# Moving the factor of an eighth from the keys into the exponential of a sparse attention kernel

## The chip, the cores and the metric

The kernel runs on one core of a Trainium2 chip. The metric is the device time of one execution in microseconds (us). The core has five engines that work side by side, each with its own queue of instructions: TensorE (PE in the views, with PEld for its weight loads), VectorE (DVE), ScalarE (ACT), GpSimd (POOL) and SyncE (SP). DMA transfers are issued from the queues of SP, ACT and POOL. An instruction that has to wait holds back everything behind it on its own queue.

## The reference

Four batches of 768 positions go through attention with 8 heads of 64 and a block-sparse mask (blocks of 32; each block of queries sees its neighbours, the first and the last block, and three sampled blocks), and then through a feed-forward layer of 512 to 2048 to 512 with a gate.

```python
scores = (1.0 / np.sqrt(64)) * np.matmul(q, k.transpose(0, 1, 3, 2))      # an eighth
scores = np.where(mask, scores, -1000000000.0)
scores = scores - np.max(scores, axis=-1, keepdims=True)
attn = np.exp(scores)
attn = attn / (np.sum(attn, axis=-1, keepdims=True) + 1e-09)
out = np.matmul(attn, v)                       # then x = out, heads side by side
h = x @ w_in
g = h * erf(softplus(h))
result = g @ w_out
```

## The kernel before

**Units.** A batch is cut into 15 units of attention: 11 of kind "m" (two blocks of queries each, all heads; the names `s_m`, `less_m`, `pf_m`, `p_m`, `pT_m`) and 4 of kind "f" (the first and the last block of queries against all keys, one pair of heads each; the names with `_f`). So there are 44 and 16 in all. `scores` (line 612) has TensorE multiply queries and keys into one PSUM tile `s`. `soft_max` (line 557) has VectorE take the negated maximum `less` of each group of `s`: four numbers per partition for an m unit, one for an f unit. `soft_exp` (line 565) has ScalarE compute exp(s + less) into `pf`, four instructions for an m unit and one for an f unit, and then a copy of `pf` in half precision, `p`; `soft_low` (line 601) gives the rest of it, and a transposing DMA issued by SP turns it for `values`, which multiplies with the values on TensorE into `po`.

**The feed-forward steps.** Between the units run 96 steps: `h` on TensorE, then on ScalarE a chain of five activations on `x` and `y`, on VectorE `y<-y,x`, on ScalarE `y<-y`, on VectorE `y<-y,h` (the gate, which is the last reader of `h` and frees one of its three buffers) and two instructions for `g`; then `o` on TensorE, and twice in eight steps an activation that takes `o` out to SBUF (`wi<-o`, `wo<-o`). From the fourth of these steps on, the engines keep the order in which the program is written (`held`, line 29 onward). Ahead of that, a stretch of some 130 us in which weights are decoded and the first units run, a scheduler puts the instructions of PE, ACT and DVE in an order of its own from its own estimate of times; SP and POOL keep the program's order all along.

**The next batch.** While a batch runs, `behind` (line 852) prepares the next one, piece by piece, once per unit. On POOL this is, in this order: the maximum over partitions for the values' scale (`allm_v`, a PARTITION_ALL_REDUCE), two gathers for the running batch, a MEMSET of `vn`, then four times `kx<-kr` with two more MEMSETs between them. `kr` is one pair of heads' keys as they come from memory; `load_k` (line 123) issues its DMA from ACT's queue into a buffer named `pf`, of which there are two, shared with the exponentials' `pf`. `order_k` (line 134) writes the keys block by block into `kx` and multiplies them by an eighth: ACT does it for batch 0, POOL for the other three. The second `kr` of a batch takes the buffer of the first one, so ACT's DMA issue for it stands in ACT's queue until POOL's first `kx<-kr` is done, and all of ACT's work behind it stands too.

All engine instructions are issued through one helper, so that they carry line 48 in the views; a group is told by its tiles.

Of the kernel before, what the change touches and what calls it, by code (L numbers as in the profile page):

```python
# [12 lines left out]
AF = mybir.ActivationFunctionType  # L13
ALU = mybir.AluOpType
# [17 lines left out]
def sparse_attention_moe(ctx: ExitStack, tc: tile.TileContext, qT, kT, v, sampled, w_in, w_out, out):  # L32
# [7 lines left out]
    class InOrder:  # L40
# [15 lines left out]
    pe, act, dve, pool, sp = (  # L56
        InOrder(e, queued if e in (nc.sync, nc.gpsimd) else held) for e in (nc.tensor, nc.scalar, nc.vector, nc.gpsimd, nc.sync)
    )
    B, H, D, S = qT.shape
# [38 lines left out]
    kxs = {}  # L98
# [35 lines left out]
    def order_k(b, pr):  # L134
        if b not in kxs:
            kxs[b] = ld.tile([P, NB, HP, BLOCK], F32, tag="kx", name=f"kx_{b}", bufs=2)
        kr = krs.pop((b, pr)).rearrange("p (n c) -> p n c", c=BLOCK)
        if b == 0:
            act.activation(kxs[b][:, :, pr, :], kr, AF.Copy, scale=D**-0.5)
        else:  # L140
            pool.tensor_scalar(kxs[b][:, :, pr, :], kr, D**-0.5, None, ALU.mult)

# [412 lines left out]
    def soft_max(unit):  # L557

        s, groups, width = softs[unit]
        tag = "_".join(str(x) for x in unit)  # L560
        less = st.tile([P, 4], F32, tag="less", name=f"less_{tag}")[:, :groups]
        dve.tensor_reduce(less, s.rearrange("p (g w) -> p g w", w=width), AX.X, ALU.max, negate=True)
        softs[unit] += (less,)

    def soft_exp(unit, early=False):

        s, groups, width, less = softs[unit]
        tag = "_".join(str(x) for x in unit)
        n = groups * width
        pf = at.tile([P, 1024], F32, tag="pf", name=f"pf_{tag}", bufs=2)[:, :n]  # L570
        for g in range(groups):
            c = slice(g * width, (g + 1) * width)
            act.activation(pf[:, c], s[:, c], AF.Exp, bias=less[:, g : g + 1])
        if early:
            softs[unit] = (s, groups, width, pf)
            return
        p2 = at.tile([P, 2048], F16, tag="p2", name=f"p2_{tag}", bufs=2)[:, : 2 * n]
        p3 = p2.rearrange("p (g a w) -> p g a w", a=2, w=width)
        pf3 = pf.rearrange("p (g w) -> p g w", w=width)
        act.activation(p3[:, :, 0], pf3, AF.Copy, scale=P_SCALE)  # L580
        softs[unit] = (p2, p3, pf3, n)
# [270 lines left out]
    def behind(m):  # L852

        for c in range(1, B):
            e = m - v_from[c]
            if e in (0, 6):
                load_v(c, 0)
            if e in (1, 3):
                max_v(c, e // 2)
            if e == 4:  # L860
                scale_v(c)
            if e in (4, 5):
                split_v(c, 1, e - 4)
            if e in (7, 8):
                split_v(c, 0, e - 7)
            if e == 8:
                have_v.add(c)
            n = m - k_from[c]
            if 1 <= n < 5:
                order_k(c, n - 1)  # L870
            if 0 <= n < 4:
                load_k(c, n)
            if n == 4:
                have_k.add(c)
# [35 lines left out]
    for pr in range(HP):  # L910
        order_k(0, pr)
# [26 lines left out]
    for begun in range(FIRST):  # L938
        with tc.high_priority():
            if begun >= 2:  # L940
                place = seen(units[begun - 2])
                values(*place)
                used_values(place)
                norm(*place)
                turn(*place, True)
            unit = units[begun]
            scores(unit)
            used_keys(unit)
            soft_max(unit)
            next_queries(begun)  # L950
            soft_exp(unit, True)
            soft_turn(unit)
        gathers()
        later(3)
        if 0 < begun < B:
            zero_rows(begun)
        if begun < 4:
            behind(begun)
# [16 lines left out]
    for m in range(len(groups) + FF_LAG):  # L975
# [39 lines left out]
        if unit:  # L1015
            soft_max(unit)
# [4 lines left out]
        if unit:  # L1021
            soft_exp(unit)
# [42 lines left out]
```

## Time and profile before

| | us |
|---|---|
| median of 3 runs | 784.99 |
| the three runs | 794.81, 779.62, 784.99 |
| the profiled execution | 783.25 |
| its span, first to last instruction | 781.5 |
| PE busy | 685.4 (88%) |
| ACT busy | 591.5 (76%) |
| DVE busy | 570.1 (73%) |
| POOL busy | 219.0 (28%) |
| mean granted TensorE clock | 0.962 of full speed |

The span is what the traced instructions cover; 1.75 us of the execution's 783.25 us lie outside it. Busy shares are means over stages with different limits, so the sections below go by stretches. In a row of the timeline the first number is the start, the second the duration, both in us; brackets at its end give the idle time of that engine just before and what ended it.

### The profile page before, as it was taken

Reading aid. Unit: us, or ns where it says so; the run is one execution under the profiler, and the core shown is the slowest. Engines: PE = TensorE matmul, PEld = TensorE weight load, DVE = VectorE, ACT = ScalarE, POOL = GpSimd, SP = SyncE. Lnnn points to the kernel's source line nnn. Section 1 sums busy time; section 2 is a strip of 40 time slices with the busy share of each in tenths; the row PEclk is TensorE's granted clock in tenths of the full one; section 3 lists DMA queues with packets and bytes.
Section 4 is the critical chain, followed back from the end, with each engine's and each line's share of the span. In section 5 each row is a group of like instructions: output and inputs, shape, how many; then the busy total and the mean of one; then the engine's idle time right before and its main releaser. Section 6 shows DMA issues by size and latency. Waiting matters only on the chain.

```text
span 781.5 us, 24790 instructions
## 1 busy us (share of the span) xinstructions
PE 685.4 (88%) x10400; PEld 449.5 (58%) x10400; DVE 570.1 (73%) x1062; ACT 591.5 (76%) x1023; POOL 219.0 (28%) x413
## 2 busy tenths in 40 slices
PE   1438578879969999899899999899899999999997
PEld 0313346556646666566566666566566666666663
DVE  6985998977748787587768877767767777664553
ACT  2546689859857887688788876888878888787774
POOL 3025523223444322222433332232533320000000
PEclk9967889999989999999999999999999999999999
DMA  9999635996499999862997997745988777221000
GB/s 318 408 276 269 194 96 112 225 205 169 120 217 185 198 178 214 198 168 56 204 199 153 231 200 143 198 112 139 223 161 190 165 139 163 56 52 25 8 28 27
DMA packets 188047, 129.35 MB, mean 166 GB/s; under 512 B 137760, under 2 KB 160928, under 8 KB 186912
## 3 DMA queue, kind: packets, MB, share of 16 engines
q1 hardware_dynamic: 173584, 84.50, 51.3%
q10 hardware_dynamic: 8464, 25.43, 10.1%
q0 software_dynamic: 5888, 17.84, 9.3%
q8 instruction: 81, 1.33, 0.7%
q14 instruction: 30, 0.25, 0.1%
HBM read 82.81 MB, written 12.95 MB: 123 GB/s over the span
## 4 chain that ended last, share of the span: by engine, by line
PE 65%; issue 9%; DMA 8%; ACT 7%; DVE 5%; POOL 4%; SPq 1%; ACTq 1%; POOLq 0%; DVEq 0%
PE h L48 28%; PE o L48 25%; PE s_m L48 5%; PE po_None L48 3%; ACT x L48 3%; DMA wo<-in_w_in_dram 2%; POOL vbuf L48 2%; PE s_f L48 2%; DVE room L48 1%; DMA kr<-in_kT_dram 1%; ACT y L48 1%; DMA raw<-in_w_out_dram 1%; PE po L48 1%; DVE wo L48 1%; DMA pT_f<-p_f 1%
## 5 line engine op out<-in xcount | busy, mean ns | idle before, releaser
L48 PE MATMUL h<-xT,wi 128*128 128x256 f16 x2304 | 272.7, 276 | 9.4 <-DVE y L48 9.4
L48 PE MATMUL o<-wo,g 128*128 128x512 f16 x1152 | 267.9, 383 | 5.4 <-ACT wi L48 5.1
L48 PEld LDWEIGHTS <-wi 128*128 128x128 f16 x2304 | 223.6, 99 | 51.0 <-issue 11.0
L48 ACT ACTIVATE x<-x 128x512 f32<-128x512 f32 x288 | 181.2, 630 | 8.9
L48 PEld LDWEIGHTS <-g 128*128 128x128 f16 x1152 | 110.1, 98 | 134.8 <-issue 17.1
L48 POOL DMA_INDIRECT vbuf<-vtab,idx x88 | 96.1, 1092 | 242.6 <-PE po_None L48 152.1
L48 DVE SCALAR_TENSOR_TENSOR y<-y,x 128x512 f32<-128x512 f32 x96 | 67.7, 705 | 90.2 <-ACT x L48 90.2
L48 ACT ACTIVATE x<-h,isg 128x512 f32<-128x512 f32 x96 | 65.2, 679 | 65.2 <-PE h L48 51.9
L48 POOL COPY kbuf<-kx 128x128 f32 (+1 forms) x280 | 86.8, 355 | 34.4 <-PE s_m L48 27.8
L48 ACT ACTIVATE y<-y 128x512 f32<-128x512 f32 x96 | 59.6, 621 | 32.7 <-DVE y L48 25.3
L48 ACT ACTIVATE pf_m<-s_m,less_m 128x256 f32<-128x256 f32 x176 | 68.3, 470 | 13.1 <-DVE less_m L48 13.1
L48 DVE SCALAR_TENSOR_TENSOR g<-y,sums,g 128x512 f16<-128x512 f32 x96 | 74.7, 778 | 3.4
L48 DVE TENSOR_REDUCE less_m<-s_m 128x4 f32<-128x1024 f32 x44 | 53.6, 1218 | 20.0 <-PE s_m L48 20.0
L48 DVE SCALAR_TENSOR_TENSOR y<-y,h 128x512 f32<-128x512 f32 x96 | 65.3, 680 | 0.3 <-ACT y L48 0.3
L48 ACT ACTIVATE y<-x 128x512 f32<-128x512 f32 x96 | 60.5, 630 | 3.0
L48 PEld LDWEIGHTS <-pT_m 128*32 128x32 f16 x3168 | 34.5, 97 | 29.4 <-issue 27.7
L48 DVE TENSOR_SCALAR g<-y,sums 128x512 f16<-128x512 f32 x96 | 48.7, 507 | 3.4
L48 POOL TENSOR_SCALAR kx<-kr 128x768 f32<-128x768 f32 x12 | 27.0, 2252 | 84.3 <-DMA kr<-in_kT_dram 61.6
L48 DVE SCALAR_TENSOR_TENSOR p_m<-pf_m,p_m 128x1024 f16<-128x1024 f32 x38 | 46.5, 1223 | 4.6 <-ACT p_m L48 4.5
L48 PE MATMUL po_None<-vbuf,pT_m 128*32 128x65 f16 (+2 forms) x3168 | 41.3, 204 | 8.8 <-issue 8.3
L48 PE MATMUL rest<-wi,room 128*128 128x512 f32 (+1 forms) x48 | 29.1, 736 | 20.9 <-ACT wi L48 8.8
L48 DVE TENSOR_TENSOR x<-xf,x 128x256 f16<-128x256 f32 x44 | 18.7, 424 | 37.3 <-ACT x L48 37.2
(108 smaller groups left out, 635.0 us busy)
## 6 DMA issues: line engine op xcount, KB each, us to landing
vbuf<-vtab SPq DMA_DIRECT2D x80, 195.0 KB, 5.1
vraw<-in_v_dram ACTq DMA_DIRECT2D x9, 768.0 KB, 5.7
vtab<-vn SPq DMA_DIRECT2D x16, 390.0 KB, 4.2
vbuf<-vtab SPq DMA_DIRECT2D x12, 520.0 KB, 6.4
wo<-in_w_out_dram ACTq DMA_DIRECT2D x6, 1024.0 KB, 9.0
qt<-in_qT_dram SPq DMA_DIRECT2D x20, 256.0 KB, 6.2
kr<-in_kT_dram ACTq DMA_DIRECT2D x12, 384.0 KB, 4.0
vbuf<-vtab SPq DMA_DIRECT2D x32, 130.0 KB, 5.1
```

The costliest lines, as they stand in the source:

```text
L48: done = call(*args, **kwargs)
```

## The change

The keys are no longer multiplied by an eighth: ACT copies them for batch 0, and POOL copies them for the others (`tensor_copy` in place of `tensor_scalar`). The scores are then eight times as large, and the factor comes in later: the exponential becomes exp(s/8 + less), with the eighth as the instruction's scale, and `less` is multiplied by an eighth by one new VectorE instruction per unit, directly behind the maximum. The result is mathematically the same.

```diff
@@ order_k
         if b == 0:
-            act.activation(kxs[b][:, :, pr, :], kr, AF.Copy, scale=D**-0.5)
+            act.activation(kxs[b][:, :, pr, :], kr, AF.Copy)
         else:
-            pool.tensor_scalar(kxs[b][:, :, pr, :], kr, D**-0.5, None, ALU.mult)
+            pool.tensor_copy(kxs[b][:, :, pr, :], kr)
@@ soft_max
         dve.tensor_reduce(less, s.rearrange("p (g w) -> p g w", w=width), AX.X, ALU.max, negate=True)
+        dve.tensor_scalar(less, less, D**-0.5, None, ALU.mult)
@@ soft_exp
-            act.activation(pf[:, c], s[:, c], AF.Exp, bias=less[:, g : g + 1])
+            act.activation(pf[:, c], s[:, c], AF.Exp, bias=less[:, g : g + 1], scale=D**-0.5)
```

**POOL, where batch 1 is prepared.** These are POOL's rows from the values' maximum to the last piece of keys, in the kernel before; a row named ISA alone is an instruction that the program's text does not contain.

```order
L48 ISA allm_v_2107<-top_v_2105 128x1
L48 DMA vbuf_106<-vtab_113,idx 96x1040
L48 DMA vbuf_107<-vtab_113,idx 96x1040
L48 MEMSET vn_1_0_2307 128x12x2
L48 ISA
L48 TENSOR_SCALAR kx_2314<-kr_0_2109 128x24x32
L48 MEMSET vn_1_1_2467 128x12x2
L48 TENSOR_SCALAR kx_2314<-kr_1_2316 128x24x32
```

And the same place in the changed kernel.

```order
L48 ISA allm_v_2117<-top_v_2115 128x1
L48 DMA vbuf_106<-vtab_113,idx 96x1040
L48 DMA vbuf_107<-vtab_113,idx 96x1040
L48 MEMSET vn_1_0_2318 128x12x2
L48 COPY kx_2325<-kr_0_2119 128x24x32
L48 MEMSET vn_1_1_2479 128x12x2
L48 COPY kx_2325<-kr_1_2327 128x24x32
```

The unnamed instruction ahead of the first piece of keys is gone, here and for batches 2 and 3, where another one ahead of `allm_v` is gone as well: five on POOL in all. The four pieces are of the form COPY.

**VectorE, one unit in the part with a fixed order** (unit 3 of batch 1; `x` from `xf` is the rest of a normalised output, `y<-y,x` and `y<-y,h` belong to the feed-forward steps). Before:

```order
L48 TENSOR_REDUCE less_m_3_3746<-s_m_3_3687 128x4
L48 TENSOR_TENSOR x_1_0_3749<-xf_0_3742,x_1_0_3749 128x256
L48 SCALAR_TENSOR_TENSOR y_1_7_3661<-y_1_7_3661,x_1_7_3657 128x512
L48 SCALAR_TENSOR_TENSOR y_1_6_3454<-y_1_6_3454,h_1_6_3425 128x512
```

And changed:

```order
L48 TENSOR_REDUCE less_m_3_3764<-s_m_3_3705 128x4
L48 TENSOR_SCALAR less_m_3_3764<-less_m_3_3764 128x4
L48 TENSOR_TENSOR x_1_0_3768<-xf_0_3760,x_1_0_3768 128x256
L48 SCALAR_TENSOR_TENSOR y_1_7_3679<-y_1_7_3679,x_1_7_3675 128x512
L48 SCALAR_TENSOR_TENSOR y_1_6_3471<-y_1_6_3471,h_1_6_3442 128x512
```

The new instruction stands directly behind its maximum and ahead of all that followed; nothing else of the fixed part moves.

**ScalarE, in the stretch ahead of the fixed order** (the exponentials `pf` and the turned copies `pT` of units 1 and 2 of batch 0; `sq` are squares of weights, `raw` and `wo` loads of weights that ACT issues). Before:

```order
L48 ACTIVATE pT_m_0_328<-turned 128x2x256
L48 ACTIVATE sq_i_394,sums<-wi 128x1024
L48 ACTIVATE pf_m_1_431<-s_m_1_396,less_m_1_429 128x256 x4
L48 ACTIVATE pT_m_1_436<-turned 128x2x256 x2
L48 DMA raw_284<-in_w_out_dram 128x1024
L48 ACTIVATE sq_i_473,sums<-wi 128x1024
L48 ACTIVATE sq_i_486,sums<-wi 128x1024
```

And changed:

```order
L48 ACTIVATE pT_m_0_329<-turned 128x2x256
L48 ACTIVATE sq_i_395,sums<-wi 128x1024
L48 DMA raw_284<-in_w_out_dram 128x1024
L48 ACTIVATE pf_m_1_433<-s_m_1_397,less_m_1_430 128x256 x4
L48 ACTIVATE sq_i_475,sums<-wi 128x1024
L48 ACTIVATE pT_m_1_438<-turned 128x2x256 x2
L48 ACTIVATE sq_i_488,sums<-wi 128x1024
```

The load of weights now stands ahead of unit 1's exponentials. The orders of ACT, DVE and PE differ in this manner through the whole opening stretch, up to where the first feed-forward steps run; behind it ACT's and PE's orders are the same in both kernels, and so is SP's throughout.

## Rows read from the trace of the kernel before

**Rows 1.** Stretches of the span: busy time of each engine, granted clock, DMA
```profile
core 0: us, PE busy (x) PEld busy (x) DVE busy (x) ACT busy (x) POOL busy (x), PEclk, DMA share, GB/s
80.00:100.00 20.00, 12.52 (x267) 7.03 (x256) 19.51 (x45) 12.64 (x25) 9.68 (x17) 0.83 0.54 175
150.00:182.00 32.00, 26.66 (x347) 16.85 (x345) 23.47 (x48) 21.52 (x37) 10.42 (x9) 0.95 0.98 213
250.00:282.00 32.00, 32.00 (x556) 21.47 (x544) 26.37 (x48) 28.95 (x52) 11.18 (x24) 1.00 1.01 205
...
322.50:326.90 4.40, 4.38 (x13) 1.69 (x13) 4.18 (x10) 2.56 (x5) 2.11 (x1) 0.61 0.93 258
```

**Rows 2.** Chain that ended last, in order of time: start, length, what
```profile
155.29 7.50 issue
162.78 2.18 POOL kx L48
...
308.70 7.28 issue
...
476.22 7.69 issue
```

**Rows 3.** Timeline, ACT: a load of keys; its first work behind the later loads
```profile
149.94 0.35 ACTq L48 DMA_DIRECT2D kr<-in_kT_dram  x1
...
165.37 0.69 ACT L48 ACTIVATE x<-h,isg 128x512 f32<-128x512 f32 x1 [4.27 <-POOL kx L48]
...
175.35 0.69 ACT L48 ACTIVATE x<-h,isg 128x512 f32<-128x512 f32 x1 [3.14 <-POOL kx L48]
...
318.57 0.69 ACT L48 ACTIVATE x<-h,isg 128x512 f32<-128x512 f32 x1 [4.04 <-POOL kx L48]
...
486.50 0.69 ACT L48 ACTIVATE x<-h,isg 128x512 f32<-128x512 f32 x1 [4.46 <-PE h L48]
```

**Rows 4.** Timeline, PE: where it stood in the same three stages
```profile
173.59 4.24 PE L48 MATMUL h<-xT,wi 128*128 128x256 f16 x24 [4.55 <-DVE y L48]
...
322.52 4.44 PE L48 MATMUL o<-wo,g 128*128 128x512 f16 x12 [2.36 <-ACT wi L48]
...
490.46 4.44 PE L48 MATMUL o<-wo,g 128*128 128x512 f16 x12 [2.77 <-ACT wi L48]
```

**Rows 5.** Timeline, POOL: an all-reduce and copies at the start; batch 1's second keys
```profile
10.88 1.29 POOL L48 PARTITION_ALL_REDUCE room<-room  x1 [10.04 <-DVE ix_room L48]
13.89 4.47 POOL L48 COPY kbuf<-kx 128x256 f32<-128x256 f32 x16 [1.72 <-ACT kx L48]
...
172.61 2.32 POOL L48 TENSOR_SCALAR kx<-kr 128x768 f32<-128x768 f32 x1 [5.44 <-DMA kr<-in_kT_dram]
```

**Rows 6.** POOL's copies: mean of the longer form; min/median/max of all
```profile
L48 POOL COPY kbuf<-kx 128x256 f32<-128x256 f32 x16 | 8.7, 542 | 2.0 <-ACT kx L48 1.7
...
L48 POOL COPY kbuf<-kx x280: 279/289/1365, 13.9 to 621.8; 128x128 f32 x124, 128x256 f32<-128x256 f32 x16
```

**Rows 7.** Timeline, DVE: an instruction on four columns, and one that reads it
```profile
440.76 0.15 DVE L48 TENSOR_SCALAR rinv_None<-po_None 128x4 f32<-128x4 f32 x1
440.95 0.18 DVE L48 RECIPROCAL rinv_None<-rinv_None 128x4 f32<-128x4 f32 x1
```

**Rows 8.** Waits, sums over the span: engine and tile, releaser, us, times, longest
```profile
DVE x L48 <- ACT x L48: 37.2, 32, 3.2
...
ACT pf_m L48 <- DVE less_m L48: 13.1, 9, 6.0
```

**Rows 9.** Timeline, ACT in the opening stretch: unit 1's exponentials, the load behind
```profile
31.98 1.53 ACT L48 ACTIVATE pf_m<-s_m,less_m 128x256 f32<-128x256 f32 x4
...
37.44 0.46 ACTq L48 DMA_DIRECT2D raw<-in_w_out_dram  x1
```

**Rows 10.** Timeline, DVE in the opening stretch: reading the sums of units 1 and 3
```profile
80.68 0.16 DVE L48 TENSOR_SCALAR rinv_None<-po_None 128x4 f32<-128x4 f32 x1
...
101.60 0.15 DVE L48 TENSOR_SCALAR rinv_None<-po_None 128x4 f32<-128x4 f32 x1
```

## The prediction

> **What bounds the kernel now.** I read the stretches first [rows 1]. In most of the fixed part TensorE is the limit: from 250 to 282 us it is busy 32.00 of 32.00 us at full clock, and whatever VectorE, ScalarE or POOL lose there is lost behind it. Two kinds of stretch are different. In the opening stretch VectorE is the limit (19.51 of 20 us busy from 80 to 100 us). And where the next batch is prepared, TensorE has holes: 26.66 of 32 us from 150 to 182, and the other engines aren't full either, so something waits.
>
> The chain in order of time says on what [rows 2]. At 155.29 us it stands for 7.50 us in "issue" on POOL, ahead of the first `kx<-kr`, and then in that instruction; the same again at 308.70 (7.28 us) and 476.22 (7.69 us): once for each of batches 1, 2 and 3. Nothing that the profile shows is waited for there, and the order of POOL has an unnamed instruction in just this place. I take it for the loading of the code that TENSOR_SCALAR needs on POOL.
>
> What hangs on it is ScalarE [rows 3]. Its queue holds the DMA issue of the second `kr`, which needs the buffer that the first `kx<-kr` reads. So ScalarE stands 4.27 us before 165.37, 4.04 before 318.57 and 4.46 before 486.50. The last one is put down to PE, but the `h` that it reads is one group older than the one that had just ended, and the chain has POOL's `kx` directly ahead of it, as in the other two. Batch 1 has a further wait of 3.14 us before 175.35, for the second piece of keys.
>
> TensorE pays for these stalls a little later [rows 4]: it stands 4.55, 2.36 and 2.77 us for buffers that ScalarE and VectorE free late. After each hole its next work is slow, 4.24 and twice 4.44 us; over one such piece the granted clock is 0.61 [rows 1], so it ran mostly at the lower of its two levels (1.2 GHz) after standing still. That is 4.40 x (1 - 0.61) = 1.7 us lost each time.
>
> **The change, part by part.**
>
> *POOL's loading goes.* Without the unnamed instruction the first copy can start at 155.3 us, when the MEMSET ahead of it has ended, if the keys have landed. They were issued at 149.94 [rows 3]; the second piece took from 164.98 to 172.61, 7.6 us, to land [rows 5], which would make it 157.5. The copy's price is not in the trace for this form. The nearest rows are POOL's own copies [rows 6]: 128 columns take 0.289 us (median), 256 take 0.542, so 0.00198 us a column, and 768 columns 0.542 + 512 x 0.00198 = 1.56 us. The bounds: 768 x 1.365/128 = 8.2 us, if all went like the slowest copy of 128 columns, and 768 x 0.00198 = 1.5 with no fixed part at all. I take 1.6, from the rows that are nearest in form, against the multiply's 2.2. The first copy then ends by 159.1 us. ScalarE comes to its DMA issue at 165.37 - 4.27 = 161.1, so its wait is gone with 2 us to spare. In batches 2 and 3 the copy ends near 310.3 and 477.8 and ScalarE comes at 314.5 and 482.0: gone too.
>
> The second wait of batch 1 mostly stays. Its DMA is issued 3.9 us earlier, but ScalarE comes earlier by as much as well; only the shorter copy (2.32 to 1.6) helps, 0.7 us, of which I count 0.5.
>
> How much of that reaches the end? In each of the three stages the chain goes from POOL through ScalarE and VectorE into TensorE, so the end moves by what ScalarE moves, until another path takes over. TensorE's own path allows more: holes and slow clock together are 4.55 + 1.7, 2.36 + 1.7 and 2.77 + 1.7, that is 6.3, 4.1 and 4.5 us. The sum is 4.8 (4.27 + 0.5) + 4.0 + 4.5 = **13.3 us gained**. The low end is 0: at 8.2 us a copy the first waits shrink only to about 2.3 us each, a gain of 6, and the second one in batch 1 grows by 5 or more. The high end is TensorE's 14.9.
>
> Of such a load the Trainium skill (GPSIMD Engine Reference, 2.1 Instruction dispatch) says that the first call of a freshly loaded kernel pays about 6 us which no profile instruction shows. The trace has 7.3 to 7.7 us in the same place, so it agrees in kind; by the page's 6 us, an estimate, a load that stayed would have POOL's copy done at 162.9 and leave ScalarE a wait of 1.8 us per batch. The sum does without it, since it goes by ScalarE's measured waits.
>
> *The two other unnamed instructions* ahead of `allm_v` in batches 2 and 3 are priced at nothing: they run while POOL waits for the values' maximum.
>
> *Sixty multiplies on VectorE.* The nearest row is TENSOR_SCALAR on four columns, 0.15 us; what reads its result starts 0.19 us after it [rows 7]. I take 0.2 us for ScalarE's start behind a maximum and 0.25 us of VectorE's time, since the multiply has to let the maximum finish first. The bounds: nothing where it is covered, and 60 x 0.25 = 15 us if every one lay on the path. What covers it: in the fixed part the next on VectorE's queue is `x<-xf,x`, which stood 32 times of 44 for ScalarE, 1.2 us on average [rows 8]; ScalarE waited for a unit's maximum only 9 times of 44; and TensorE covers the rest wherever it is full. Without that cover it costs 0.25 us a unit. I count two exposed places, 2 x 0.2 = 0.4 us. In the opening stretch VectorE is the limit, and there the six units' multiplies count in full: 6 x 0.25 = 1.5 us.
>
> *ScalarE's scales* (four copies without one, 192 exponentials with one) are priced at nothing: ScalarE has slack except in the stages above, where 1 to 2 exponentials lie on the chain. That scale and bias are one fused step ahead of the function is what the Trainium skill says (ScalarE: Activation LUTs, Step-by-step); no run here shows an exponential both ways.
>
> *The opening stretch's new order* can go either way. The clearest loss: the load of weights that started at 37.44 us now stands ahead of unit 1's exponentials, which ran at 31.98 [rows 9], so they slip by some 5.9 us if the load can't start sooner. I take that as hidden, because what fills VectorE there is the decoding of weights, which needs nothing from the units. The bounds are half a unit's spacing either way: units follow each other by (101.60 - 80.68)/2 = 10.5 us [rows 10], so -5 to +5. I take 0.
>
> **The sum.** The profiled execution took 783.25 us, 1.7 less than the median of 784.99. 783.25 - 13.3 + 0.4 + 1.5 = 771.9, so **772 us**, 1.7% below the median. About 2% is what a measurement of this kernel can tell from no change; that is 769.3 and 800.7 us.
>
> **Rivals.**
>
> *The next wait takes the place (0.17).* In each stage the second `kr`, the writes of `vn` or the turned `p` come next, and half of the gain goes into them. For it: 175.35 waits 3.14 us for a landing that doesn't get shorter. Against it: batches 2 and 3 show no second wait of ScalarE in their stages. 783.25 - 6.6 + 1.9 = 778.5.
>
> *The opening goes better (0.13).* The new order lets the weights be ready half a unit earlier, 5 us: 767. For it: VectorE is nearly full there and any hole that closes counts. Against it: the same instructions and six more.
>
> *The opening loses (0.10), the other side.* In the new order the weight loads on ScalarE's queue stand behind exponentials that now need one more VectorE instruction; if such a load misses its place, the decoding falls back by a unit's spacing, 10.5 us: 782.4. It decides from 11.4 us on, where the gain is eaten; with two units, 21 us, it is 793, slower than before. For it: the order of three engines changes. Against it: the loads come mainly from memory, and the slip that [rows 9] shows has cover.
>
> *No gain (0.05).* COPY needs its own code after the all-reduce, and the load only changes its name; or the slow bound of the copy holds. 783.25 + 1.9 = 785. Against it: at the start POOL goes from an all-reduce that ends at 12.17 us to copies at 13.89, and those 1.72 us are a wait for ScalarE's `kx` [rows 5]. (It is what the rule of the Trainium skill on first calls, GPSIMD Engine Reference, 2.1, would make of it.)
>
> **How the numbers follow.** The forecast has 0.55, with its own range of 766 to 778: the copy's and the second wait's bounds, the clock, and a few us of the opening's order. About 0.14 of that lies under 769.3; with the better opening this is 0.27 for faster by over 2%. Over 800.7 us only an opening that loses more than two units would end, 0.04. The rest, 0.69, is within 2%. The range takes in the forecast's, the next wait, most of the better opening and the opening that loses one unit: 764 to 784; about 1 in 10 is left out on either side.
>
> **What would show it.** Right: POOL's COPY `kx` starts within 3 us of the MEMSET ahead of it, at about 1.6 us each; no wait of ScalarE for `kx` over 0.5 us in batches 2 and 3, one of about 2.5 in batch 1; TensorE's granted clock at 1.00 through these stages with no pieces of 4.4 us; the multiply at about 0.16 us. Wrong: copies over 2.5 us, or a gap of 6 to 8 us ahead of the first one; the fixed part beginning more than 5 us earlier or later; ScalarE's waits for `less` well over 13 us.

## The result, and the profile after

The changed kernel took 773.93 us (median of 6 executions, 769.97 to 778.98) beside 785.19 us for the kernel before, a ratio of 0.9867 with a 95% interval of 0.9822 to 0.9912. Measured a second time beside other kernels it came to 775.42 against 786.73 us, 0.9894 (0.9849 to 0.9940). So it is 1.1 to 1.3% faster, 8 to 10 us, within the 2% that was called "no change". Ratios leave disturbed executions out on both sides, so they aren't exactly the quotient of the medians beside them.

| | before | changed |
|---|---|---|
| profiled execution | 783.25 | 778.98 |
| span | 781.5 | 777.2 |
| a second profiled execution | | 773.26 (span 771.5) |
| mean granted clock | 0.962 | 0.974; second 0.967 |

The first profiled execution of the changed kernel is the slowest of its six, so a second one stands beside it wherever it reads differently. Busy times of the page of the changed kernel (us, share of the span, number of instructions):

```profile
PE 689.9 (89%) x10400; PEld 451.6 (58%) x10400; DVE 577.2 (74%) x1122; ACT 591.6 (76%) x1023; POOL 201.0 (26%) x413
```

POOL has 18 us less to do, VectorE 7 more. The groups that the change made (operation, tile, shape, count | busy us, mean ns | idle before):

```profile
L48 POOL COPY kx<-kr 128x768 f32<-128x768 f32 x12 | 12.1, 1012 | 58.4 <-DMA kr<-in_kT_dram 58.4
L48 DVE TENSOR_SCALAR less_m<-less_m 128x4 f32<-128x4 f32 x44 | 7.8, 178 | 1.2
L48 DVE TENSOR_SCALAR less_f<-less_f 128x1 f32<-128x1 f32 x16 | 2.5, 154 | 0.6
```

ScalarE's exponentials of the m units take 470 ns each without the scale (before) and 472 ns with it (changed):

```profile
L48 ACT ACTIVATE pf_m<-s_m,less_m 128x256 f32<-128x256 f32 x176 | 68.3, 470 | 13.1 <-DVE less_m L48 13.1
...
L48 ACT ACTIVATE pf_m<-s_m,less_m 128x256 f32<-128x256 f32 x176 | 68.8, 472 | 24.1 <-DVE less_m L48 22.8 <-DVE room L48 1.0 <-PE po_None L48 0.2
```

**POOL.** Its timeline answers [rows 2] and [rows 5]. The first piece of keys of each batch is copied directly behind the MEMSET, where 7.28 to 7.69 us had stood:

```profile
149.11 0.13 POOL L48 MEMSET vn<- 128x24 f16 x1
149.18 0.83 POOL L48 COPY kx<-kr 128x768 f32<-128x768 f32 x1
161.96 0.12 POOL L48 MEMSET vn<- 128x24 f16 x1 [11.95 <-DVE less_f L48]
162.01 1.10 POOL L48 COPY kx<-kr 128x768 f32<-128x768 f32 x1
...
304.74 0.83 POOL L48 COPY kx<-kr 128x768 f32<-128x768 f32 x1
...
473.76 0.83 POOL L48 COPY kx<-kr 128x768 f32<-128x768 f32 x1
```

**ScalarE.** The timeline that answers [rows 3]: behind each load of keys the first activation `x<-h` follows with no wait in brackets, in all three batches, and behind the second load of batch 1 too:

```profile
153.69 0.33 ACTq L48 DMA_DIRECT2D kr<-in_kT_dram  x1
155.75 0.67 ACT L48 ACTIVATE x<-h,isg 128x512 f32<-128x512 f32 x1
163.78 0.33 ACTq L48 DMA_DIRECT2D kr<-in_kT_dram  x1
165.38 0.67 ACT L48 ACTIVATE x<-h,isg 128x512 f32<-128x512 f32 x1
...
311.31 0.67 ACT L48 ACTIVATE x<-h,isg 128x512 f32<-128x512 f32 x1
...
480.34 0.67 ACT L48 ACTIVATE x<-h,isg 128x512 f32<-128x512 f32 x1
```

**TensorE.** Against [rows 4]: the pieces of 4.44 us in the stages of batches 2 and 3 are 2.75 us now. In the stage of batch 1 a hole ahead of `h` is left, and behind it a piece slower than before:

```profile
166.87 5.28 PE L48 MATMUL h<-xT,wi 128*128 128x256 f16 x24 [3.41 <-DVE y L48]
...
316.89 2.75 PE L48 MATMUL o<-wo,g 128*128 128x512 f16 x12
...
485.91 2.75 PE L48 MATMUL o<-wo,g 128*128 128x512 f16 x12
```

The stretches say the same ([rows 1] has 150 to 182 us at a clock of 0.95 and the 4.40-us piece at 0.61):

```profile
core 0: us, PE busy (x) PEld busy (x) DVE busy (x) ACT busy (x) POOL busy (x), PEclk, DMA share, GB/s
140.00:172.00 32.00, 28.03 (x426) 18.49 (x424) 27.99 (x56) 23.58 (x42) 6.34 (x9) 0.91 1.11 214
...
315.00:319.50 4.50, 4.50 (x24) 2.41 (x23) 4.32 (x10) 2.58 (x5) 0.94 (x2) 1.00 0.82 166
```

And the waits beside [rows 8]: ScalarE stands longer for the maxima than before (13.1 us), VectorE's `x` a little less for ScalarE (37.2):

```profile
ACT pf_m L48 <- DVE less_m L48: 22.8, 11, 6.1
...
DVE x L48 <- ACT x L48: 31.2, 31, 3.3
```

**Where the time went.** Each feed-forward step begins on ScalarE with one activation `x<-h,isg`, 96 in all, so its start is a milestone that every timeline has. The table compares them with the profiled execution of before, where steps 5, 12, 24, 28, 48, 52 and 95 start at 151.41, 205.61, 298.12, 332.22, 465.63, 499.86 and 766.39 us. "Opening" is the lead at step 5; "stage 1, 2, 3" is what it changes by from step 5 to 12, 24 to 28 and 48 to 52; "rest" is all that lies between and behind; minus is earlier than before. The kernels are those of the next section.

| profiled execution | opening | stage 1 | stage 2 | stage 3 | rest | step 95 |
|---|---|---|---|---|---|---|
| changed | -5.8 | -0.4 | -3.4 | -3.3 | +8.6 | -4.2 |
| e5, changed again | -5.9 | -3.5 | -3.3 | -3.3 | +6.1 | -10.0 |
| e1, no multiply | -2.9 | -1.9 | -3.7 | -3.7 | 0.0 | -12.2 |
| e2, loading stays | -7.0 | +0.5 | -0.2 | +4.5 | +0.1 | -2.1 |
| e3, three multiplies | -0.8 | -1.0 | -3.4 | -2.6 | +1.0 | -6.8 |
| e4, batch 0 as before | -2.8 | -2.1 | -3.3 | -2.6 | +2.0 | -8.9 |
| e6, multiply in opening | -4.8 | -1.9 | -3.6 | -2.3 | +3.0 | -9.6 |
| e7, split behind gate | -2.2 | -1.0 | -3.5 | -3.4 | +1.6 | -8.6 |
| e8, scaled queries | +0.7 | -1.9 | -3.6 | -2.9 | +3.3 | -4.4 |
| e9, load put back | -3.8 | -0.9 | -1.5 | -1.2 | +4.5 | -3.0 |
| e10, e4 again | -2.0 | -2.0 | -3.4 | -2.7 | +2.3 | -7.7 |
| e11, values earlier | -0.9 | +0.5 | -3.3 | -3.6 | -3.3 | -10.6 |
| e12, second split | -3.5 | -2.6 | -3.3 | -3.2 | +5.6 | -6.9 |

The eight executions without POOL's loading and with the values' work in its place (all but e2, e9 and the three that move that work, e7, e11 and e12) gain 1.8, 3.4 and 2.9 us in the three stages on average, 8.2 in sum. Stage 1 alone goes from 0.4 to 3.5 among them, and there is one profiled execution of the kernel before to compare with. Opening and rest scatter by several us between executions of one and the same order (changed and e5: 8.6 and 6.1 us given back; one hole of 3.26 us ahead of `s_m` at 396.35 us, for which the first trace names nothing, is not there in the second).

### The profile page after: what moved, and what is told of

Read it like the earlier page. It is cut to its first block, busy times and chain, and to the rows that moved or that the text cites. A ratio compares the mean times of both kernels' runs of the same rounds, so it can differ in the third digit from the quotient of the medians.

```text
span 777.2 us, 24891 instructions
## 1 busy us (share of the span) xinstructions
PE 689.9 (89%) x10400; PEld 451.6 (58%) x10400; DVE 577.2 (74%) x1122; ACT 591.6 (76%) x1023; POOL 201.0 (26%) x413
## 3 DMA queue, kind: packets, MB, share of 16 engines
q10 hardware_dynamic: 8464, 25.43, 10.4%
## 4 chain that ended last, share of the span: by engine, by line
PE 66%; DVE 11%; ACT 9%; DMA 7%; issue 4%; SPq 1%; ACTq 1%; DVEq 0%
PE h L48 28%; PE o L48 26%; PE s_m L48 6%; PE po_None L48 3%; ACT x L48 3%; PE s_f L48 2%; DVE room L48 2%; DMA vbuf<-vtab 2%; DMA vtab<-vn 1%; DVE y L48 1%; DVE xf L48 1%; DVE less_m L48 1%; ACT y L48 1%; ACT pf_m L48 1%; PE po L48 1%
## 5 line engine op out<-in xcount | busy, mean ns | idle before, releaser
L48 ACT ACTIVATE pf_m<-s_m,less_m 128x256 f32<-128x256 f32 x176 | 68.8, 472 | 24.1 <-DVE less_m L48 22.8
L48 DVE SCALAR_TENSOR_TENSOR g<-y,sums,g 128x512 f16<-128x512 f32 x96 | 73.0, 760 | 3.4
L48 PE MATMUL s_m<-kbuf,qt 64*32 64x160 f32 x1408 | 49.7, 319 | 5.1 <-issue 4.3
L48 PE MATMUL s_m<-kx,qt 64*32 64x96 f32 x1408 | 30.9, 260 | 24.9 <-ACT kx L48 13.0
```

Of the source, the lines that this page charges most:

```text
L48: done = call(*args, **kwargs)
```

## The experiments

The medians and ratios, each against the kernel before beside it:

| kernel | us | before | ratio | 95% interval |
|---|---|---|---|---|
| e1, no multiply | 771.44 | 781.88 | 0.9888 | 0.9837 to 0.9939 |
| e2, loading stays | 781.42 | 781.88 | 0.9994 | 0.9958 to 1.0029 |
| e3, three multiplies | 773.97 | 781.88 | 0.9889 | 0.9851 to 0.9928 |
| e4, batch 0 as before | 777.11 | 781.88 | 0.9943 | 0.9909 to 0.9977 |
| e5, changed again | 775.42 | 786.73 | 0.9894 | 0.9849 to 0.9940 |
| e6, multiply in opening | 773.17 | 786.73 | 0.9851 | 0.9796 to 0.9906 |
| e7, split behind gate | 775.16 | 786.73 | 0.9898 | 0.9842 to 0.9953 |
| e8, scaled queries | 778.54 | 786.73 | 0.9901 | 0.9866 to 0.9938 |
| e9, load put back | 780.84 | 787.96 | 0.9944 | 0.9910 to 0.9977 |
| e10, e4 again | 775.89 | 787.96 | 0.9887 | 0.9828 to 0.9947 |
| e11, values earlier | 773.10 | 787.96 | 0.9856 | 0.9800 to 0.9912 |
| e12, second split | 773.73 | 787.96 | 0.9839 | 0.9780 to 0.9899 |

### POOL's part and VectorE's part, each alone

e1 takes the multiply and the scale out of the changed kernel, so that its computation leaves the eighth out:

```diff
-        dve.tensor_scalar(less, less, D**-0.5, None, ALU.mult)
...
-            act.activation(pf[:, c], s[:, c], AF.Exp, bias=less[:, g : g + 1], scale=D**-0.5)
+            act.activation(pf[:, c], s[:, c], AF.Exp, bias=less[:, g : g + 1])
```

> Alone the POOL part of the change: the keys are copied, and neither the multiply of the maxima nor the exponential's scale is there, so the eighth is left out of the computation. The order on TensorE, VectorE and ScalarE is that of the kernel before, in the opening stretch too. Against a kernel before of 785 us. Theory A, the sum of the prediction (the three stalls are worth 13.3 us, the opening's new order nothing, the multiplies 1.9): 772 us, with the feed-forward steps after stage 3 some 13 us earlier than before. Theory B (the opening's new order has given 6 us, and the multiplies have eaten 7 to 8 in the fixed part): 772 to 774 us too, but the opening at the time of before, and none of the stages' gain given back between them. Theory C (the next wait takes the place of the stalls whatever VectorE does): 778 us or more, with the gain of each stage given back behind it as in the changed kernel.

e2 puts POOL's TENSOR_SCALAR back into the changed kernel and leaves the rest:

```diff
-            pool.tensor_copy(kxs[b][:, :, pr, :], kr)
+            pool.tensor_scalar(kxs[b][:, :, pr, :], kr, 1.0, None, ALU.mult)
```

> The rest of the change without the POOL part: POOL multiplies the keys by 1.0 with TENSOR_SCALAR, so the loading stays; the multiplies, the exponential's scale and the opening's new order are those of the changed kernel. Theory A: 785 + 1.9 = 787 us, the first feed-forward step within 2 us of before. Theory B: the first step 6 us earlier, 7 to 8 us given back later: 785 to 787 us. Theory C: 6 us earlier in the opening and nothing given back but by the stages: 779 to 780 us.

POOL's part alone is worth 1.12% (8.8 us), VectorE's part with the opening's new order 0.06% (0.5 us, between 3.3 gained and 2.3 lost). The product of both, 0.9882, lies between the two measurements of the whole change, 0.9867 and 0.9894. So the gain is POOL's. In e2 ScalarE stands where it stood before; its timeline in the stages of batches 1 and 2:

```profile
158.36 0.69 ACT L48 ACTIVATE x<-h,isg 128x512 f32<-128x512 f32 x1 [4.21 <-POOL kx L48]
...
168.34 0.69 ACT L48 ACTIVATE x<-h,isg 128x512 f32<-128x512 f32 x1 [3.14 <-POOL kx L48]
...
315.92 0.69 ACT L48 ACTIVATE x<-h,isg 128x512 f32<-128x512 f32 x1 [3.83 <-POOL kx L48]
```

e1's 8.8 us (4.8 to 12.7 by its interval) are not the 13.3 of theory A's sum: stage 1 gives 1.9 where 4.8 were counted. Theory C's 7 us lie inside the interval, so the time alone does not rule it out; its mechanism does not fit, since nothing of the stages' gain is given back behind them in e1 (rest 0.0). In e2 theory C's 5 to 6 us of gain are outside the interval, and theory A's first step within 2 us of before is a miss: step 5 starts 7.0 us early. (In stage 3 of e2, which loses 4.5 us, TensorE stands 3.25 us for ScalarE's `y` ahead of the loading, with slow pieces behind; what held ScalarE there stays open.)

### The loading, or the shorter copy?

e9 puts a tiny TENSOR_SCALAR ahead of the first copy of each batch:

```diff
+            if pr == 0:
+                tiny = st.tile([P, 1], F32, tag="tiny", name=f"tiny_{b}")
+                pool.memset(tiny, 0.0)
+                pool.tensor_scalar(tiny, tiny, 1.0, None, ALU.mult)
             pool.tensor_copy(kxs[b][:, :, pr, :], kr)
```

> The changed kernel, with a MEMSET and a TENSOR_SCALAR by 1.0 on one column on POOL ahead of each batch's first copy of keys (three of each, the result the same). POOL's order has the unnamed instruction in its old place again, three times, while the copies keep their new form. If the loading was the cause: 7.3 to 7.7 us of nothing ahead of these three TENSOR_SCALARs, ScalarE stands 4.0 to 4.5 less the 1.2 us by which the copy is shorter, some 3 us, three times, and 6 to 7 of the 9 us of gain are gone: 2 to 3 us under before. If the shorter copy was the cause: 8 to 9 us under before, as the changed kernel.

4.4 us under before (1.8 to 7.1), where 2 to 3 or 8 to 9 were expected: about half of the gain is gone. The ratio's interval overlaps the changed kernel's, but all twelve executions of e9 (778.36 to 785.73 us) are slower than all twelve of e11 and e12 (768.34 to 777.75), which ran beside it without the loading; so the loading does cost time. POOL's timeline has the old gap ahead of an instruction on one column:

```profile
158.33 0.46 POOL L48 TENSOR_SCALAR tiny<-tiny 128x1 f32<-128x1 f32 x1 [7.55 <-issue]
158.74 0.82 POOL L48 COPY kx<-kr 128x768 f32<-128x768 f32 x1
...
311.70 0.26 POOL L48 TENSOR_SCALAR tiny<-tiny 128x1 f32<-128x1 f32 x1 [7.29 <-issue]
...
479.79 0.26 POOL L48 TENSOR_SCALAR tiny<-tiny 128x1 f32<-128x1 f32 x1 [7.52 <-issue]
```

and ScalarE's has the stalls, the three first ones shorter by 1.2 to 1.6 us (the copy takes 0.8 us where the multiply took 2.2) and batch 1's second one by 0.5:

```profile
159.97 0.69 ACT L48 ACTIVATE x<-h,isg 128x512 f32<-128x512 f32 x1 [3.09 <-POOL kx L48]
...
169.82 0.69 ACT L48 ACTIVATE x<-h,isg 128x512 f32<-128x512 f32 x1 [2.66 <-POOL kx L48]
...
313.16 0.69 ACT L48 ACTIVATE x<-h,isg 128x512 f32<-128x512 f32 x1 [2.62 <-POOL kx L48]
...
481.24 0.69 ACT L48 ACTIVATE x<-h,isg 128x512 f32<-128x512 f32 x1 [2.86 <-POOL kx L48]
```

So the gap belongs to TENSOR_SCALAR, whatever its size, and not to the keys; it stood behind an all-reduce each time, and no run has it without one. That it is the loading of code is read from the unnamed instruction in that place; no row shows the loading itself. The stages keep 3.7 us of their 8.2 in e9; that would be the shorter copies' part, by one execution. The Trainium skill (GPSIMD Engine Reference, 2.1 Instruction dispatch) gives about 6 us for the first call of freshly loaded code; the six gaps of before and of e9 are 7.28 to 7.69 us, and the measured number decides.

### What a multiply costs

e3 has three multiplies by a half in place of one in the part with a fixed order, e6 none there, so that the eighth is left out of those units' computation:

```diff
e3:
-        dve.tensor_scalar(less, less, D**-0.5, None, ALU.mult)
+        for part in (0.5, 0.5, 0.5) if held[0] else (D**-0.5,):
+            dve.tensor_scalar(less, less, part, None, ALU.mult)
e6:
-        dve.tensor_scalar(less, less, D**-0.5, None, ALU.mult)
+        if not held[0]:
+            dve.tensor_scalar(less, less, D**-0.5, None, ALU.mult)
...
-            act.activation(pf[:, c], s[:, c], AF.Exp, bias=less[:, g : g + 1], scale=D**-0.5)
+            act.activation(pf[:, c], s[:, c], AF.Exp, bias=less[:, g : g + 1], scale=1.0 if held[0] else D**-0.5)
```

> The changed kernel with three multiplies by a half in place of one by an eighth for each of the 52 units in the part with a fixed order (104 more instructions on VectorE, the result the same; the opening stretch as in the changed kernel). Theory A (a multiply is hidden but in two places): 774 + 2 x 2 x 0.2 = 775 us. Theory B (each multiply costs 0.15 to 0.2 us wherever TensorE seems full): 774 + 104 x 0.15 to 0.2 = 790 to 795 us. Theory C: 774 to 775 us.

> The changed kernel with the multiply and the exponential's scale in the opening stretch alone: the units of the part with a fixed order leave the eighth out of the computation. The orders are those of the changed kernel. Theory D: 10 + 5 = 14 to 15 us under before, some 5 under the changed kernel. Theory E: 8 us under before, as the changed kernel.

104 multiplies more move the ratio from 0.9894 to 0.9889, 0.4 us the other way. The half-widths of the two intervals are 3.0 and 3.6 us, together 4.7 (the root of the sum of squares), so a multiply costs at most 0.04 us. Theory B's 790 to 795 us is out. e6, with 52 fewer, is 3.4 us under e5 (0.9851 against 0.9894), which is inside the intervals; its 11.7 us under before (7.4 to 16.0) lie between theory E's 8 and theory D's 14 to 15 and rule out neither. VectorE's fifty-two multiplies in the fixed part are hidden, as near as this can be measured; the eight in the opening stretch are measured only together with its new order (e2). e5, the changed kernel once more, was measured beside e6:

> The changed kernel once more, beside the others on one chip and with a second profile. Theory D, from the runs so far (POOL's part is worth 9 to 10 us, the opening's new order 4 to 5, and the multiplies cost 4 to 5 in the part with a fixed order): 10 us under before. Theory E (only POOL's part counts, and it is worth 8; the rest is scatter between executions): 8 us under before. For both: TensorE's hole of 3 to 4 us in stage 1, ended by VectorE's y, is there again, and the one of 3.3 us ahead of s_m near 396 us, for which the profile names nothing, is not.

It came out at 8.3 us (4.7 to 11.9, which takes in D's 10 and E's 8), with the hole in stage 1 at 2.32 us, where 3 to 4 were expected, and without the hole near 396 us.

### The opening's order

e4 leaves batch 0 as it was, which keeps the opening's order of before; e10 is e4 once more.

```diff
-            act.activation(kxs[b][:, :, pr, :], kr, AF.Copy)
+            act.activation(kxs[b][:, :, pr, :], kr, AF.Copy, scale=D**-0.5)
...
-        dve.tensor_scalar(less, less, D**-0.5, None, ALU.mult)
+        if unit[1]:
+            dve.tensor_scalar(less, less, D**-0.5, None, ALU.mult)
...
-            act.activation(pf[:, c], s[:, c], AF.Exp, bias=less[:, g : g + 1], scale=D**-0.5)
+            act.activation(pf[:, c], s[:, c], AF.Exp, bias=less[:, g : g + 1], scale=D**-0.5 if unit[1] else 1.0)
```

> The change for batches 1 to 3 alone: ScalarE goes on scaling the keys of batch 0, whose 15 units have no multiply and no scale in the exponential; 45 multiplies are left, all in the part with a fixed order. The opening stretch has the order of before. Theory A: 774 - 1.5 = 772 to 773 us. Theory B: the opening's 6 us are lost and 15 multiplies of 0.15 to 0.2 us saved: 774 + 6 - 2.5 = 777 to 778 us. Theory C: 780 us.

> Once more the change for batches 1 to 3 alone (batch 0's keys scaled by ScalarE, 45 multiplies, the opening's order of before), which came out 4.5 us under before where the copy without any multiply came out 8.8 under. If the difference was scatter: 8 to 9 us under before. If the opening's order of before costs 4 to 5 us beside multiplies: 4 to 5 us under before again.

e4 came out 4.5 us under before, from which I made theory D (the new order gives 4 to 5 us, the multiplies take them). e10 came out 8.9 us under before: the same kernel, so the two differ by scatter, and what theory D was built on is gone. Its other half, multiplies that take 4 to 5 us (0.08 to 0.10 us for each of 52), is above e3's bound of 0.04. What the order itself is worth stays unsettled. Step 5 is 4.2 us ahead of before on average over the eight profiled executions with the new order (0.8 to 7.0; changed, e2, e3, e5, e6, e7, e9 and e12 in the table; e11 has the values' work earlier in its opening and is left out), and 1.4 over the five with the old (from 0.7 late to 2.9 early, before itself with 0), but e2, 7.0 us ahead at step 5, is no faster as a whole.

### The next wait in stage 1

In stage 1 TensorE's `h` waits for VectorE's gate `y<-y,h`. Ahead of the gate on VectorE's queue stand two instructions on `vn`, the lower half of a split of the next batch's values, which read what ScalarE's `vn` writes. ScalarE and then VectorE in the changed kernel, ahead of TensorE's `h` at 166.87 us (VectorE's wait is put down to nothing here; in e5 it is 2.04 us, for ScalarE's `vn`):

```profile
164.37 1.10 ACT L48 ACTIVATE vn<-vraw,s_v 128x384 f16<-128x384 f32 x2
...
165.07 1.15 DVE L48 SCALAR_TENSOR_TENSOR vn<-vraw,s_v,vn 128x384 f16<-128x384 f32 x2 [1.42 <-issue]
166.13 0.68 DVE L48 SCALAR_TENSOR_TENSOR y<-y,h 128x512 f32<-128x512 f32 x1
```

e7 puts this part of three splits, and the write that follows it, behind the next gate; e12 does so for the second split alone; e11 begins the values of batch 1 a unit earlier.

```diff
e7 (in e12 the first line is "if not (b and quad and half):"):
-            dve.scalar_tensor_tensor(lo, vr, s, hi, ALU.mult, ALU.subtract)
+            if not (b and (quad or not half)):
+                dve.scalar_tensor_tensor(lo, vr, s, hi, ALU.mult, ALU.subtract)
+            else:
+                put_off.append(lambda lo=lo, vr=vr, hi=hi: dve.scalar_tensor_tensor(lo, vr, s, hi, ALU.mult, ALU.subtract))
...
+        if put_off:
+            put_off.append(write)
+        else:
+            write()
...
             ff_gate(*last)
+        while put_off:
+            put_off.pop(0)()
e11:
-    v_from = {c: 6 if c == 1 else c * per - 9 for c in range(1, B)}
+    v_from = {c: 5 if c == 1 else c * per - 9 for c in range(1, B)}
```

> The changed kernel with VectorE's part of three of the four splits of a batch's values (two instructions of 0.57 us each on vn, and the write that follows them) put behind the gate y<-y,h of the next feed-forward step. Theory F (in stage 1 VectorE's vn, which waits for ScalarE's vn, stands ahead of the gate, and TensorE's h waits for the gate): the hole of 3.2 to 3.4 us falls to about 1.7, since the gate can then start when ScalarE's y ends, 1.7 us earlier; 2 to 3 us under the changed kernel. Rival (ScalarE's exponentials set the hole): it stays over 3 us and the time with it.

> The changed kernel with VectorE's part of the second split of a batch's values alone put behind the gate of the next feed-forward step, and nothing else moved. In the run with three splits put off, the first one's write came later, and ScalarE's second vn stood 3.41 us for it. Theory F: with the first split in its place that wait is gone, and so is TensorE's hole of 2.3 to 3.4 us ahead of h: 2 to 4 us under the changed kernel. If the wait moves again (to po, whose pT is turned by a DMA of 5.4 us in the same stretch): the same time as the changed kernel, with a hole ahead of po in stage 1.

> The changed kernel with the preparation of batch 1's values begun one unit earlier (five units in place of six), the keys as they are; the result the same. If stage 1's hole comes from the splits of the values meeting the f units' work on VectorE and ScalarE, it falls under 2 us, and the slow piece behind it goes: 2 to 4 us under the changed kernel. If the work only meets other work one unit earlier: the same time, with the hole there. It is also a try at a better version.

The hole ahead of `h` goes in e7, but its time is that of e5. ScalarE's timeline shows why: the first split's write now comes later, and the second `vn`, which uses the same buffer, waits for it:

```profile
169.12 1.12 ACT L48 ACTIVATE vn<-vraw,s_v 128x384 f16<-128x384 f32 x2 [3.41 <-DMA vtab<-vn]
```

and TensorE stands later, ahead of `po`:

```profile
166.51 2.79 PE L48 MATMUL h<-xT,wi 128*128 128x256 f16 x24
...
177.87 1.50 PE L48 MATMUL po_None<-vbuf,pT_m 128*32 128x65 f16 x72 [4.68 <-issue]
```

e12 leaves the first split in its place, and TensorE's hole is gone with nothing slow behind it; a wait of 2.59 us comes up ahead of `po` (0.77 us before), and the slow piece now stands behind that one:

```profile
165.54 2.78 PE L48 MATMUL h<-xT,wi 128*128 128x256 f16 x24 [0.18 <-DVE y L48]
...
174.79 0.90 PE L48 MATMUL po_None<-vbuf,pT_m 128*32 128x65 f16 x72 [2.59 <-issue]
175.63 4.46 PE L48 MATMUL h<-xT,wi 128*128 128x256 f16 x24
```

Its stage 1 gains 2.6 us, inside the 0.4 to 3.5 of the kernels that leave the splits alone; e7's gains 1.0, and e11's loses 0.5. In e11 the hole in the old place shrinks to 0.23 us, and another stands 25 us later, with its slow piece:

```profile
168.46 2.78 PE L48 MATMUL h<-xT,wi 128*128 128x256 f16 x24 [0.23 <-DVE y L48]
...
192.96 4.45 PE L48 MATMUL h<-xT,wi 128*128 128x256 f16 x24 [3.79 <-DVE y L48]
```

So theory F's cause is shown for the hole ahead of `h`, and that the wait moves on when it is taken away: none of the three shows the 2 to 4 us that this was to bring. e12 and e11 have the lowest ratios beside e6's (0.9839, 0.9856), but their intervals overlap the changed kernel's: neither is shown to be better than it.

### The eighth in the queries

e8 has no multiply at all: POOL copies, and ScalarE scales the queries of batches 1 to 3 in place. Against the kernel before:

```diff
-            pool.tensor_scalar(kxs[b][:, :, pr, :], kr, D**-0.5, None, ALU.mult)
+            pool.tensor_copy(kxs[b][:, :, pr, :], kr)
...
+        if b and n < NU - 1 and n % 2 == 1:
+            act.activation(qts[b, n // 2 + 1], qts[b, n // 2 + 1], AF.Copy, scale=D**-0.5)
+        if n == NU + 1 and b + 1 < B:
+            act.activation(qts[b + 1, 0], qts[b + 1, 0], AF.Copy, scale=D**-0.5)
```

> The kernel before with POOL copying the keys, and the eighth multiplied into the queries of batches 1 to 3 by 18 instructions of ScalarE (128 x 512 each, in place, one unit ahead of their use); batch 0 as before; no multiply of the maxima, no scale in the exponential, the result the same. The opening's order is that of before. Theory D: as without any multiply, 9 to 10 us under before, if the 18 instructions (0.4 to 0.5 us each by the nearest rows of ScalarE, x at 0.64 for 128 x 512) are hidden where TensorE is full. Theory E: 8 us under before. Rival: each of them counts, 18 x 0.5 = 9 us, and nothing is left of the gain.

It is 7.8 us under before, as the changed kernel is. ScalarE's 18 instructions took 11.0 us in all and are hidden too, as far as its 4.9 to 10.7 us can tell (the rival's loss of 9 us is out):

```profile
L48 ACT ACTIVATE qt<-qt 128x512 f32<-128x512 f32 x18 | 11.0, 614 | 0.0
```

## Why the prediction was right

772 us, a gain of 11.4 us against the profiled execution, came near to the 10.4 and 8.3 us by the two ratios (11.3 between the medians, both times), and the mechanism is shown by e1, e2 and e9. The terms were less good than their sum.

- **The loading and ScalarE's three first stalls**: right. The gap belongs to TENSOR_SCALAR (e9), COPY needs none, and the stalls are gone.
- **The copy's price**: 1.6 us was too high; it took 0.82 to 1.41 us. No harm, since the copy has ended 3.7 us before ScalarE comes to the next load (149.18 + 0.83 against 153.69). (The low bound, a copy of 8.2 us, counted a wait of 2.3 us in batch 1 too; with the landing at 157.5 that stands beside it, it would have been 4.6.)
- **The second wait of batch 1**, of which about 2.5 us were to stay: wrong. It is gone as well. ScalarE came to its third load 10.1 us after the second (153.69 to 163.78), where in the kernel before it hurried through a backlog and came after 7.2 (from 164.98 to 172.2, the 175.35 of [rows 3] less its wait of 3.14). The first stall had made the second; e9, which brings back the first, has the second too (2.66 us).
- **The sum of 13.3 us**: this is the step that failed. It let the end move by what ScalarE moves, because TensorE's holes allowed more; the stages gave 8.2. Its largest miss is stage 1, 4.8 counted and 1.8 won on average: there the hole had a second holder, the gate behind VectorE's `vn`, and most of it stays. TensorE's own rows give the size. Before, 4.55 of hole and 1.46 of slowness (4.24 against 2.78) are 6.0; in e1 3.17 and 1.67 are 4.8. That is 1.2 us, and the wait of 0.77 us ahead of the next `po` is gone as well: 2.0, where the milestones show 1.9. In the first profiled execution of the changed kernel, 3.41 and 2.50, and 0.44 more in the next piece (`s_f` at 1.90 for 1.46), are 6.35: nothing gained but the 0.8 at `po`, and 0.4 shown. In stages 2 and 3 the terms of 4.0 and 4.5 did reach TensorE: with the hole ahead of `o` and the slow piece behind it gone, 4.2 and 4.6 us are won there in e5, as in every profiled execution without the loading. But 0.87 and 1.80 us are given back some 15 us ahead of that place, in the scores `s_m`, which take 2.0 and 3.0 us up to the next `o` in place of 1.1, with small holes that the profile names nothing for, at a granted clock of 1.00 (464 to 467 us); with what else shifts, 3.4 and 3.1 us are left. In e5:

```profile
301.12 0.75 PE L48 MATMUL s_m<-kbuf,qt 64*32 64x160 f32 x20 [0.26 <-issue]
...
465.81 0.48 PE L48 MATMUL s_m<-kbuf,qt 64*32 64x160 f32 x5 [0.30 <-issue]
466.55 0.54 PE L48 MATMUL s_m<-kbuf,qt 64*32 64x160 f32 x11 [0.25 <-issue]
```

  In e1, e3 and e4 `s_m` is as fast as before within 0.12 us, and 0.4 to 1.5 us are lost at the `h` behind the following `po`; e2, which has the loading, loses 1.0 there in stage 2 too, so this loss need not come from the change. Its cause stays open. The sum priced it at nothing.
- **The multiplies**: 0.170 us each in the median (0.151 to 0.282), near the 0.15 of the row that they were priced by, and the 1.9 us for them were too much rather than too little: e2 has 0.5 us of gain, e3 no slope. The opening holds eight of them, not the six that were counted. ScalarE's wait for `less` did grow from 13.1 to 22.8 us, which I had named as a sign of being wrong, but e6, which multiplies in the opening alone, has 17.6, e1 with the old order 14.5, and the time follows none of them.
- **ScalarE's scales**: at nothing, as priced. The prediction had no exponential both ways; the two kernels' rows now show 470 and 472 ns.
- **The opening**: taken at nothing with 5 us either way. Step 5 of the feed-forward came 5.8 and 5.9 us early in the two profiled executions, past my sign for "wrong", and what was won there was given back behind it.
- **The rivals**: "the next wait takes the place" is what stage 1 did; in stages 2 and 3 what was given back stood elsewhere than it named. "No gain" is out (e1), and so is an opening that loses (e2). "The opening goes better" is open: step 5 is early in every profiled execution with the new order, and no time shows the gain.

The sum's 5.1 us too many in the stages and its 1.9 us for VectorE, against 0.5 gained, cancel in part, and this is why 772 came out as well as it did: luck, not a better sum.

## What to carry to other kernels

Before an engine's stall is counted as gain, look at the hole that it leaves on the engine that sets the end, and ask who else would have ended that hole and when: only the difference is won. On POOL, choose operations by what code they need, not by their own duration: a TENSOR_SCALAR on one column stood behind a gap of 7.3 to 7.6 us after an all-reduce, and a copy in its place, with the factor moved elsewhere, had no such gap. Small instructions on an engine with slack (sixty of 0.17 us on VectorE, 18 of 0.61 on ScalarE) took that factor at no cost that could be measured here.

## What the hardware showed that I had not expected

- A hole of one length can be followed by either clock. The stage 1 of e5 and of e9, TensorE's stretch behind a hole of 2.32 and of 2.28 us (its first 24 matmuls on `h` took 2.78 and 4.45 us). e5:

```profile
core 0: us, PE busy (x) PEld busy (x) DVE busy (x) ACT busy (x) POOL busy (x), PEclk, DMA share, GB/s
...
166.00:170.00 4.00, 3.54 (x27) 2.79 (x27) 3.89 (x7) 2.98 (x6) 0.28 (x1) 1.00 1.10 233
```

and e9:

```profile
168.00:173.00 5.00, 4.45 (x25) 3.38 (x25) 3.27 (x4) 3.05 (x5) 0.82 (x1) 0.66 1.10 230
```

  The granted clock stayed at its upper level (2.4 GHz) in the one and was at the lower (1.2 GHz) for most of the piece in the other. This alone is 1.67 us of difference between two executions; what decides it was not tried.
- POOL's copy does not cost by the column as its shorter forms suggest: 0.289 and 0.542 us for 128 and 256 columns [rows 6], and 0.82 us for 768, where the slope of the two would give 1.56.
- Executions of one kernel scatter by more than the parts of this change: by 1.2% between the ends of six (769.97 to 778.98), with the opening's end (step 5) up to 6 us apart for one order. Two measurements of one kernel (e4, e10) gave 0.9943 and 0.9887.
